# Sliding-window attention with Q/K stacks in two tiles: the second tile holds tokens 768 to 2047 instead of 1024 to 2047

## The chip, the cores and the metric

The kernel is one program on one core of one Trainium2 chip. The metric is device time in microseconds (us) of one execution. Three executions of the kernel before took 1101.31, 1106.22 and 1108.74 us; their median is 1106.22.

## The reference

One transformer block on 2048 tokens of width 640: attention with 32 heads of 20 over a sliding window of 256 tokens, then a gated MLP that also mixes along the sequence. The change concerns the attention.

```
h = layernorm(x); q, k, v = split(h @ wqkv)            # 32 heads, Dh = 20
scores = q @ k.T * Dh ** -0.5
mask = (i - j >= 0) & (i - j < 256)                    # query i, key j
o = softmax(where(mask, scores, -1e9)) @ v
h = x + o @ wo
z = gelu(layernorm(h) @ w_in); z1, z2 = halves(z); g = w_sp @ layernorm(z2) + b_sp
out = h + (z1 * g) @ w_out
```

## The kernel before, in words

**Stages.** The span has four: normalization, V, Q and K (0 to about 239 us), attention (about 239 to 468 us), output projection with the second normalization, and the MLP, whose products on TensorE fill the rest.

**Q and K in pieces.** Q and K are f32 values that must keep their accuracy, so `split_qk` (lines 603 to 620) cuts each into three bf16 parts on ScalarE, VectorE and GpSimd and stores them with one DMA for each (m, c) into the DRAM tensor `qk_d`: m (0 to 9) counts blocks of 128 rows of Q and K, c (0 to 3) blocks of 512 tokens. Two bf16 tokens travel as one f32 word.

**Stacks.** A group g is four heads; there are eight. For a group `load_stack` (lines 316 to 330) fills a stack: the six products of parts that matter are laid on 6 x 20 = 120 partitions, so one bf16 matmul over 120 rows gives the f32 score. A stack has two SBUF tiles: tile 0 holds tokens 0 to 1023, tile 1 tokens 1024 to 2047, each with four heads of Q (index 0) and K (index 1). 12 DMAs of 160 KB fill a tile (line 329). Three stacks (`slot_w`, `slot_ap`) are used in turn; the third lies in the buffers `xb`, which hold the last half of the normalized input until Q and K are done, and the second in memory that the first half held. Before a stack's first use GpSimd sets the K rows 96 to 127 to ones (line 322).

**Maxima and scores.** The program needs the row maximum before the exponential. `max_item(g, qb, hh)` (line 345) computes for one head and 128 queries the scores against up to 384 keys, in four strips of 32 queries with 288 keys each (line 359), and VectorE takes the masked maximum (line 369). In the group 0, which runs in the stage before, it is one product of 128 queries with 384 keys (line 363). `max_rows(g, b)` (line 372) turns the maxima of eight query blocks with a product (line 375), cuts them into three bf16 rows on VectorE and GpSimd, stores them to the DRAM tensor `m_d` (line 384) and loads them into the partitions 120 to 122 of the stack's Q, tile b (line 386). `score_item(u, hh)` (line 391) computes, transposed, the scores of 128 keys with the 384 queries that see them, less the maxima, over 123 rows (line 412), ScalarE takes the exponential (line 415), GpSimd clears the two triangles outside the window (lines 419 and 422), and `pv_item` (line 425) multiplies by V (line 440).

**Spans over two tiles.** `tokens` (line 332) cuts a span of keys or queries that crosses token 1024 into two pieces, each with its weight load and its matmul. For each head this is so in the query blocks 8 and 9 of the maxima and in the key blocks 6 and 7 of the scores: four strips each, so 16 more weight loads and 16 more matmuls a head. The columns streamed are the same, 288 a strip.

**Order.** The attention loop (line 760) is written out by hand: step s computes the four heads of max block s + 16 and of score block s, with PV of block s - 2 between them. A group is 16 steps. SP issues all DMAs in program order; the loads of the stack for two groups ahead are spread over a group's 16 steps, tile 0 first. PE, VectorE and ScalarE also keep program order; GpSimd's order is chosen by the scheduler of the framework.

Of the kernel before, what the change touches and what calls it, by code (L numbers as in the profile page):

```python
# [7 lines left out]
F32 = mybir.dt.float32  # L8
# [26 lines left out]
def block_kernel(ctx, tc, x, xt, wqk, wv, wo, w_in, wsp, bsp, w_out, out):  # L35
# [220 lines left out]
    with ExitStack() as ab:  # L256
# [21 lines left out]
        add_slot(0, s0)  # L278
        add_slot(2, [h[:, :2 * S] for h in xb])
        mask = tmp2.tile([P, 384], BF16, name="mask")  # L280
# [35 lines left out]
        def load_stack(g):  # L316


            st = slot_w[g % 3]
            if g < 3:  # L320
                for h in st:
                    nc.gpsimd.memset(h[96:P, 1], ONES)
                    if g == 2:
                        yield
            for b in range(2):
                for j, parts in enumerate(((0, 0), (0, 1), (0, 2), (1, 0), (1, 1), (2, 0))):
                    for a in range(2):
                        src = qk_d[g // 4, parts[a], b, a * DH:(a + 1) * DH, g % 4 * 4:g % 4 * 4 + 4]
                        nc.sync.dma_start(st[b][j:6 * DH:6, a], src)
                        yield  # L330

        def tokens(st, rows, a, hh, t0, n):

            o = 0
            while o < n:
                c, t = divmod(t0 + o, S // 2)
                w = min(n - o, S // 2 - t)
                yield o, w, st[c][:rows, a, hh, t:t + w]
                o += w

        def one(st, rows, a, hh, t0, n):
            (_, _, x), = tokens(st, rows, a, hh, t0, n)
            return x

        def max_item(g, qb, hh, strips=True):

            st = slot_ap[g % 3]
            ps = s1_tile()
            lo = max(0, qb - 2) * P
            n = (qb + 1) * P - lo  # L350
            keep = mask[:, 384 - n:]
            if strips:
                skip = 32 if qb > 1 else 0
                if skip:
                    n, keep = 288, strip
                for j in range(4):
                    q0 = qb * P + 32 * j
                    for o, w, k in tokens(st, 120, 1, hh, lo + skip * j, n):
                        nc.tensor.matmul(ps[32 * j:32 * j + 32, o:o + w], one(st, 120, 0, hh, q0, 32), k,  # L359
                                         start=True, stop=True, tile_position=(0, 32 * j))  # L360
            else:
                for o, w, k in tokens(st, 120, 1, hh, lo, n):
                    nc.tensor.matmul(ps[:, o:o + w], one(st, 120, 0, hh, qb * P, P), k, start=True, stop=True)  # L363
# [27 lines left out]
        def score_item(u, hh):  # L391
# [14 lines left out]
            for i in range(4):  # L406
                k0 = kb * P + 32 * i
                b, e = 32 * i, min(n, 32 * i + 288)
                if NU - LEAD < u and 4 * (u - NU + LEAD - 1) + hh < 6:
                    b, e = 0, n  # L410
                for o, w, q in tokens(st, 123, 0, hh, kb * P + b, e - b):
                    nc.tensor.matmul(ps[32 * i:32 * i + 32, b + o:b + o + w], one(st, 123, 1, hh, k0, 32), q,  # L412
                                     start=True, stop=True, tile_position=(0, 32 * i))
            if u <= NU - LEAD:
# [50 lines left out]
        if True:  # L465
# [137 lines left out]
            def split_qk(m, c, ps):  # L603
# [10 lines left out]
                else:  # L614
                    nc.scalar.activation(sg[:, 1, :], rest, AF.Copy)  # L615
                nc.gpsimd.tensor_tensor(out=sg[:, 2, :], in0=rest, in1=sg[:, 1, :], op=OP.subtract)  # L616
                T = S // 4
# [103 lines left out]
            def dense_tail():  # L721
                split_wqk(8)
                split_wqk(9)
                for n, (m, c) in enumerate((m, c) for c in range(4) for m in (6, 7, 8, 9)):
# [3 lines left out]
                    if n == 7:  # L728
                        x01.close()
                        s1 = pool(x01, "slot1p", side="right")  # L730
                        add_slot(1, [s1.tile([P, 2 * S], F32R, name=f"slot1_{i}") for i in range(2)])
                    if n >= 7:
# [830 lines left out]
```

## Time and profile before

| what | value |
|---|---|
| median of three executions | 1106.22 us |
| the profiled execution | 1106.83 us, of which its span 1105.1 us |
| mean granted TensorE clock | 0.998 |
| attention steps: 245 to 445 us | PE busy 188.92, VectorE 183.95, ScalarE 178.65, GpSimd 135.68 of 200 us |
| end of attention: 445 to 470 us | PE 22.93, ScalarE 20.73, GpSimd 20.97 of 25 us |
| the rest: 553 to 1105 us | PE 543.51 of 552 us |
| DMA in 245 to 445 us | 35.62 MB, 16 engines busy 0.57 of the time |

PE stands for TensorE's matmuls and PEld for its weight loads, DVE for VectorE, ACT for ScalarE, POOL for GpSimd, SP for the engine that issues DMAs. An x with a number is a count. In brackets behind a row stands how long the engine was idle before it and what released it; "issue" means that the engine waited for nothing that the profile shows. A matmul's end is modelled, so consecutive matmuls overlap in the rows, and idle time of PE is counted from the modelled end.

### The profile page before, as it was taken

The numbers are of one execution on the slowest core, as the hardware profiler recorded it, in microseconds if no ns is written. First come the engines' busy times: TensorE is split into PE (matmuls) and PEld (weight loads), VectorE is DVE, ScalarE is ACT, GpSimd is POOL, SyncE is SP. The second block draws the span as 40 slices with busy tenths as digits, with TensorE's granted clock in tenths as the row PEclk, the third lists the DMA queues.
The fourth block names the chain that finished last, engine by engine and source line by source line (L and its number), as shares of the span: only waits on it lengthen the run. The fifth ranks groups of instructions, "written<-read, shape, count | busy, mean of one in ns | idle before, by whom it ended". The sixth has DMA issues, their size and how long they took to land.

```text
span 1105.1 us, 28802 instructions
## 1 busy us (share of the span) xinstructions
PE 1075.1 (97%) x11083; PEld 970.4 (88%) x11083; DVE 781.6 (71%) x2157; ACT 604.1 (55%) x1258; POOL 314.3 (28%) x447
## 2 busy tenths in 40 slices
PE   8999999999999999999999999999999999999998
PEld 7998887668777788699999999999999899999998
DVE  6643444789899999576677669655456899987784
ACT  4443443249888899846766556443448533333331
POOL 4324446677666676811300012000001000000000
PEclk9999999999999999999999999999999999999999
DMA  7833567555555555689654442242441467684642
GB/s 249 299 115 118 175 173 273 166 166 187 183 183 182 176 178 163 167 267 311 247 200 153 152 142 76 64 132 95 134 147 51 166 229 249 234 272 142 191 145 96
DMA packets 92282, 194.74 MB, mean 176 GB/s; under 512 B 11952, under 2 KB 46272, under 8 KB 88256
## 3 DMA queue, kind: packets, MB, share of 16 engines
q1 hardware_dynamic: 92144, 192.90, 53.5%
q8 instruction: 87, 1.43, 0.5%
q14 instruction: 51, 0.42, 0.1%
HBM read 127.90 MB, written 64.95 MB: 175 GB/s over the span
## 4 chain that ended last, share of the span: by engine, by line
PE 43%; DMA 4%; issue 4%; ACT 3%; DVE 3%; POOL 2%; SPq 0%; ACTq 0%; POOLq 0%; DVEq 0%
PE g L1181 23%; PE zb L1066 4%; PE out_x L1345 3%; PE zx L1006 2%; PE out_v L1345 2%; PE zv L1006 2%; DMA h_d<-xh 1%; PE zy L1006 1%; PE zw L1006 1%; PE out_y L1345 1%; PE yt L1300 1%; DMA fx<-wsp_in 1%; DVE row L822 1%; PE wo_ps L118 1%; ACT pt L417 1%
## 5 line engine op out<-in xcount | busy, mean ns | idle before, releaser
L415 ACT ACTIVATE pt<-bank 128x384 f32<-128x384 f32 (+1 forms) x452 | 179.7, 485 | 22.6 <-PE bank L412 18.5
L1181 PE MATMUL g<-zl,aw 128*128 128x432 f32 x768 | 168.9, 357 | 0.7 <-ACT zl L828 0.7
L369 DVE CUSTOM_DVE_ANT_0 junk<-bank,strip 128x288 bf16<-128x288 f32 x392 | 157.1, 452 | 14.9 <-PE bank L359 12.9
L828 ACT ACTIVATE aw<-fx 128x512 fp32r<-128x512 f32 (+2 forms) x152 | 86.0, 586 | 128.3 <-PE g L1181 53.5
L1181 PEld LDWEIGHTS g<-zl,aw 128*128 128x128 f32 x768 | 144.0, 188 | 7.0 <-ACT zl L828 1.1
L822 DVE TENSOR_TENSOR aw<-fx,aw 128x512 fp32r<-128x512 f32 (+2 forms) x152 | 95.9, 639 | 59.4 <-ACT aw L828 59.1
L440 PE MATMUL pv<-pt,v_sb 128*32 128x192 f32 (+3 forms) x1984 | 134.3, 323 | 3.3 <-issue 1.3
L1181 PE MATMUL g<-ze,aw 128*128 128x432 f32 x576 | 132.6, 359 | 2.3 <-DVE row L822 2.3
L1181 PEld LDWEIGHTS g<-ze,aw 128*128 128x128 f32 x576 | 107.1, 188 | 9.0 <-DVE row L822 3.7
L359 PE MATMUL bank<-slot 120*32 120x288 bf16 (+5 forms) x1280 | 95.9, 277 | 4.2 <-issue 2.5
L419 POOL TENSOR_SCALAR_AFFINE_SELECT pt<-pt 128x512 f32<-128x512 f32 x128 | 81.7, 639 | 56.7 <-ACT pt L415 53.5
L412 PE MATMUL bank<-slot 123*32 123x288 bf16 (+6 forms) x1296 | 96.8, 275 | 0.7 <-ACT pt L415 0.7
L412 PEld LDWEIGHTS <-slot 123*32 123x32 bf16 x1728 | 61.2, 97 | 13.5 <-issue 3.7
L422 POOL TENSOR_SCALAR_AFFINE_SELECT pt<-pt 128x512 f32<-128x512 f32 x112 | 72.8, 650 | 0.0
L440 PEld LDWEIGHTS pv<-pt,v_sb 128*32 128x32 f32 x1984 | 63.1, 110 | 10.4 <-POOL pt L419 4.8
L359 PEld LDWEIGHTS <-slot 120*32 120x32 bf16 x1440 | 51.7, 96 | 16.4 <-issue 9.6
L822 DVE TENSOR_TENSOR row<-g,row 128x432 f32<-128x432 f32 x80 | 48.4, 605 | 21.5 <-PE g L1181 21.1
L369 DVE CUSTOM_DVE_ANT_0 junk<-bank,mask 128x384 bf16<-128x384 f32 (+2 forms) x120 | 51.2, 447 | 16.8 <-PE bank L363 15.6
L616 POOL TENSOR_TENSOR sg<-rest,sg 128x512 bf16<-128x512 f32 x40 | 46.7, 1168 | 56.9 <-ACT sg L615 46.3
L606 DVE TENSOR_TENSOR rest<-qk,std 128x512 f32<-128x512 f32 x40 | 27.6, 690 | 47.8 <-PE qk L594 47.8
L608 ACT ACTIVATE sg<-rest 128x512 bf16<-128x512 f32 x40 | 25.2, 631 | 53.5 <-DVE rest L606 53.5
L118 PE MATMUL wo_ps<-xb,xb 128*128 128x320 f32 x260 | 52.4, 311 | 1.4 <-DVE mvc L1460 1.4
(263 smaller groups left out, 2528.1 us busy)
## 6 DMA issues: line engine op xcount, KB each, us to landing
slot<-qk_d SPq DMA_DIRECT2D x144, 160.0 KB
fx<-wsp_in SPq DMA_DIRECT2D x32, 512.0 KB
qk_d<-sg SPq DMA_DIRECT2D x40, 384.0 KB
o_d<-ot SPq DMA_DIRECT2D x64, 128.0 KB
xb<-qk_d SPq DMA_DIRECT2D x48, 160.0 KB
fx<-hn_d SPq DMA_DIRECT2D x24, 320.0 KB
z_d<-row SPq DMA_DIRECT2D x16, 432.0 KB
g_d<-row SPq DMA_DIRECT2D x16, 432.0 KB
```

Of the source, the lines that this page charges most:

```text
L359: nc.tensor.matmul(ps[32 * j:32 * j + 32, o:o + w], one(st, 120, 0, hh, q0, 32), k, start=True, stop=True, tile_position=(0, 32 * j))
L369: nc.vector.tensor_tensor_reduce(out=junk[:, :n], in0=ps[:, :n], in1=keep, scale=1.0, scalar=NEG, op0=OP.add, op1=OP.max, accum_out=m_cols ...
L412: nc.tensor.matmul(ps[32 * i:32 * i + 32, b + o:b + o + w], one(st, 123, 1, hh, k0, 32), q, start=True, stop=True, tile_position=(0, 32 * i))
L415: nc.scalar.activation(pt[:, hh, :n], ps[:, :n], AF.Exp, scale=SCALE)
L419: nc.gpsimd.affine_select(out=pt[:, :, :P], in_=pt[:, :, :P], pattern=[[0, 4], [1, P]], base=0, channel_multiplier=-1, compare_op=OP.is_ge ...
L422: nc.gpsimd.affine_select(out=pt[:, :, 256:], in_=pt[:, :, 256:], pattern=[[0, 4], [-1, P]], base=-1, channel_multiplier=1, compare_op=OP. ...
L440: nc.tensor.matmul(ps[32 * hh:32 * hh + 32, a - 512 * c:b - 512 * c], v_sb[:, kb, v0:v0 + 32], pt[:, hh, a - kb * P:b - kb * P], start=fir ...
L822: (eng or nc.vector).tensor_tensor(out=out, in0=a, in1=b, op=op)
L828: nc.scalar.activation(out, a, AF.Copy)
L1006: nc.tensor.matmul(ps, a[x], b[:, y], start=start and m + x + y == 0, stop=stop and m == n - 1 and x == 1, skip_group_check=True)
L1181: nc.tensor.matmul(ps, w[m][:, x, k], zc[k][m][:, y], start=start and k + x + y == 0, stop=stop and k == 3 and x == 1, skip_group_check=True)
L1345: nc.tensor.matmul(o[b][:, :HD], l[:, x, k * P:(k + 1) * P], r[k][:, y], start=start and k + x + y == 0, stop=stop and k == 2 and x == 1, ...
```

## The change

`qk_d` becomes two DRAM tensors: the first holds tokens 0 to 1023 (512 words), the second tokens 768 to 2047 (640 words). The second tile of each stack has 1280 tokens instead of 1024. Each span of keys or queries now lies in one tile: maxima use tile 0 for query blocks 0 to 7 and tile 1 from block 8, scores tile 0 for key blocks 0 to 5 and tile 1 from block 6. Tokens 768 to 1023 are stored, loaded and kept twice: `split_qk` stores the c = 1 blocks with two DMAs (ten more DMAs in all), the 12 loads of tile 1 carry 200 KB each, the maxima of query blocks 6 and 7 are loaded into both tiles (eight more DMAs), and the memset of tile 1 covers 2560 columns instead of 2048.

```diff
-    qk_d = dram.tile([2, 3, 2, 2 * DH, H // 2, S // 4], F32, name="qk_d")
+    WORDS = (S // 4, S // 4 + P)
+    qk_d = [dram.tile([2, 3, 2 * DH, H // 2, n], F32, name=f"qk_d{b}") for b, n in enumerate(WORDS)]
...
-        s0 = [s0.tile([P, 2 * S], F32R, name=f"slot0_{i}") for i in range(2)]
+        s0 = [s0.tile([P, 8 * n], F32R, name=f"slot0_{i}") for i, n in enumerate(WORDS)]
...
-        def tokens(st, rows, a, hh, t0, n):
-
-            o = 0
-            while o < n:
-                c, t = divmod(t0 + o, S // 2)
-                w = min(n - o, S // 2 - t)
-                yield o, w, st[c][:rows, a, hh, t:t + w]
-                o += w
-
-        def one(st, rows, a, hh, t0, n):
-            (_, _, x), = tokens(st, rows, a, hh, t0, n)
-            return x
+        def one(st, b, rows, a, hh, t0, n):
+            t = t0 - 6 * P * b
+            return st[b][:rows, a, hh, t:t + n]
...
+            half_b = qb // 8
...
-                    for o, w, k in tokens(st, 120, 1, hh, lo + skip * j, n):
-                        nc.tensor.matmul(ps[32 * j:32 * j + 32, o:o + w], one(st, 120, 0, hh, q0, 32), k,
-                                         start=True, stop=True, tile_position=(0, 32 * j))
+                    nc.tensor.matmul(ps[32 * j:32 * j + 32, :n], one(st, half_b, 120, 0, hh, q0, 32),
+                                     one(st, half_b, 120, 1, hh, lo + skip * j, n),
+                                     start=True, stop=True, tile_position=(0, 32 * j))
...
-            nc.sync.dma_start(slot_w[g % 3][b][120:123, 0], rows.rearrange("a (h r) c -> a h (r c)", h=4))
+            rows, st = rows.rearrange("a (h r) c -> a h (r c)", h=4), slot_w[g % 3]
+            if b == 0:
+                nc.sync.dma_start(st[0][120:123, 0], rows)
+                nc.sync.dma_start(st[1][120:123, 0, :, :P], rows[:, :, 6 * P // 2:])
+            else:
+                nc.sync.dma_start(st[1][120:123, 0, :, P:], rows)
...
-                for o, w, q in tokens(st, 123, 0, hh, kb * P + b, e - b):
-                    nc.tensor.matmul(ps[32 * i:32 * i + 32, b + o:b + o + w], one(st, 123, 1, hh, k0, 32), q,
-                                     start=True, stop=True, tile_position=(0, 32 * i))
+                c = int(kb > 5)
+                nc.tensor.matmul(ps[32 * i:32 * i + 32, b:e], one(st, c, 123, 1, hh, k0, 32),
+                                 one(st, c, 123, 0, hh, kb * P + b, e - b),
+                                 start=True, stop=True, tile_position=(0, 32 * i))
...
-                base = qk_d[m // 5, 0, c // 2, m % 5 * 8, 0, c % 2 * 256:c % 2 * 256 + 256]
-                nc.sync.dma_start(bass.AP(tensor=base.tensor, offset=base.offset,
-                                          ap=[[T, P], [2 * 2 * DH * H // 2 * T, 3], [1, 256]]), sg.bitcast(F32))
+                for b in range(2):
+                    t0, t1 = max(c * 256, 3 * P * b), min(c * 256 + 256, (3 * P + WORDS[1]) if b else WORDS[0])
+                    if t0 >= t1:
+                        continue
+                    o = t0 - 3 * P * b
+                    base = qk_d[b][m // 5, 0, m % 5 * 8, 0, o:o + t1 - t0]
+                    nc.sync.dma_start(bass.AP(tensor=base.tensor, offset=base.offset,
+                                              ap=[[WORDS[b], P], [2 * DH * H // 2 * WORDS[b], 3], [1, t1 - t0]]),
+                                      sg[:, :, 2 * (t0 - c * 256):2 * (t1 - c * 256)].bitcast(F32))
```

The first place where the instruction order differs is PE at key block 6 of group 1, head 0, in the attention loop; `bank` is a PSUM bank, `slot_0_1953` and `slot_1_1954` are the two tiles of the stack (`slot_1_1964` is tile 1 of the changed program), 32 is the strip's keys and the last number the streamed columns. Before:

```order
L412 LDWEIGHTS slot_0_1953
L412 MATMUL bank_124<-slot_0_1953 32x256
L412 LDWEIGHTS slot_0_1953
L412 MATMUL bank_124<-slot_1_1954,slot_0_1953 32x32
L412 LDWEIGHTS slot_0_1953
L412 MATMUL bank_124<-slot_0_1953 32x224
L412 LDWEIGHTS slot_0_1953
L412 MATMUL bank_124<-slot_1_1954,slot_0_1953 32x64
```

These are two of the head's four strips. In the changed program the same head is this:

```order
L410 LDWEIGHTS slot_1_1964
L410 MATMUL bank_125<-slot_1_1964 32x288
L410 LDWEIGHTS slot_1_1964
L410 MATMUL bank_125<-slot_1_1964 32x288
L410 LDWEIGHTS slot_1_1964
L410 MATMUL bank_125<-slot_1_1964 32x288
L410 LDWEIGHTS slot_1_1964
L410 MATMUL bank_125<-slot_1_1964 32x288
```

All four strips now take eight instructions where they took sixteen. Over the whole program PE has 976 instructions fewer: 488 weight loads and 488 matmuls.

The second place is GpSimd at the end of the stage before attention, where it splits the last blocks of Q and K (`rest`, `sg`) and sets the ones of the third stack's second tile (`xb_98` before, `xb_99` in the changed program). Before:

```order
L616 TENSOR_TENSOR sg_3_2268<-rest_3_2269,sg_3_2268 128x512
L322 MEMSET xb_98 32x2048
L610 TENSOR_TENSOR rest_3_2311<-rest_3_2311,sg_3_2310 128x512
L381 CAST m_0_1_2356<-mr_1_2357 32x128
L613 CAST sg_3_2310<-rest_3_2311 128x512
```

And in the changed program:

```order
L323 MEMSET xb_99 32x2560
L615 TENSOR_TENSOR sg_3_2272<-rest_3_2273,sg_3_2272 128x512
L609 TENSOR_TENSOR rest_3_2315<-rest_3_2315,sg_3_2314 128x512
L374 CAST m_0_1_2360<-mr_1_2361 32x128
L612 CAST sg_3_2314<-rest_3_2315 128x512
```

The memset is a quarter larger and stands one instruction earlier, ahead of the split of the last block but one.

The third place is SP where the maxima of the first eight query blocks of group 1 come back from DRAM. Before there is one load, `L386 DMA slot_0_1953<-m_d 3x2048`; in the changed program there are two:

```order
L381 DMA slot_0_1963<-m_d 3x2048
L382 DMA slot_1_1964<-m_d 3x4x128
```

SP has 18 DMAs more in all: these eight and the ten second stores of `split_qk`.

More of the change, by code (lines that the diff above doesn't have):

```diff
@@ L278, in block_kernel @@
         add_slot(0, s0)
-        add_slot(2, [h[:, :2 * S] for h in xb])
+        add_slot(2, [h[:, :8 * n] for h, n in zip(xb, WORDS)])
         mask = tmp2.tile([P, 384], BF16, name="mask")
@@ L327, in load_stack @@
                     for a in range(2):
-                        src = qk_d[g // 4, parts[a], b, a * DH:(a + 1) * DH, g % 4 * 4:g % 4 * 4 + 4]
+                        src = qk_d[b][g // 4, parts[a], a * DH:(a + 1) * DH, g % 4 * 4:g % 4 * 4 + 4]
                         nc.sync.dma_start(st[b][j:6 * DH:6, a], src)
                         yield
-        def tokens(st, rows, a, hh, t0, n):
-            o = 0
-            while o < n:
-                c, t = divmod(t0 + o, S // 2)
-                w = min(n - o, S // 2 - t)
-                yield o, w, st[c][:rows, a, hh, t:t + w]
-                o += w
-        def one(st, rows, a, hh, t0, n):
-            (_, _, x), = tokens(st, rows, a, hh, t0, n)
-            return x
+        def one(st, b, rows, a, hh, t0, n):
+            t = t0 - 6 * P * b
+            return st[b][:rows, a, hh, t:t + n]
         def max_item(g, qb, hh, strips=True):
@@ L357, in max_item @@
                     q0 = qb * P + 32 * j
-                    for o, w, k in tokens(st, 120, 1, hh, lo + skip * j, n):
-                        nc.tensor.matmul(ps[32 * j:32 * j + 32, o:o + w], one(st, 120, 0, hh, q0, 32), k,
-                                         start=True, stop=True, tile_position=(0, 32 * j))
-            else:
-                for o, w, k in tokens(st, 120, 1, hh, lo, n):
-                    nc.tensor.matmul(ps[:, o:o + w], one(st, 120, 0, hh, qb * P, P), k, start=True, stop=True)
+                    nc.tensor.matmul(ps[32 * j:32 * j + 32, :n], one(st, half_b, 120, 0, hh, q0, 32),
+                                     one(st, half_b, 120, 1, hh, lo + skip * j, n),
+                                     start=True, stop=True, tile_position=(0, 32 * j))
+            else:
+                nc.tensor.matmul(ps[:, :n], one(st, half_b, 120, 0, hh, qb * P, P), one(st, half_b, 120, 1, hh, lo, n),
+                                 start=True, stop=True)
             b, c = divmod(qb, 8)
@@ L616, in split_qk @@
                 nc.gpsimd.tensor_tensor(out=sg[:, 2, :], in0=rest, in1=sg[:, 1, :], op=OP.subtract)
-                T = S // 4
-                base = qk_d[m // 5, 0, c // 2, m % 5 * 8, 0, c % 2 * 256:c % 2 * 256 + 256]
-                nc.sync.dma_start(bass.AP(tensor=base.tensor, offset=base.offset,
-                                          ap=[[T, P], [2 * 2 * DH * H // 2 * T, 3], [1, 256]]), sg.bitcast(F32))
+                for b in range(2):
[7 more added lines that the diff above has]
+                                      sg[:, :, 2 * (t0 - c * 256):2 * (t1 - c * 256)].bitcast(F32))
             halves = [slice(0, HD), slice(HD, D)]
@@ L730, in dense_tail @@
                         s1 = pool(x01, "slot1p", side="right")
-                        add_slot(1, [s1.tile([P, 2 * S], F32R, name=f"slot1_{i}") for i in range(2)])
+                        add_slot(1, [s1.tile([P, 8 * n], F32R, name=f"slot1_{i}") for i, n in enumerate(WORDS)])
                     if n >= 7:
```

## The prediction

> **What bounds the kernel now.** I read the page first, then the stretches of the attention stage, then who waited for whom there, then the single waits.
>
> ```profile
> span 1105.1 us, 28802 instructions
> PE 1075.1 (97%) x11083; PEld 970.4 (88%) x11083; DVE 781.6 (71%) x2157; ACT 604.1 (55%) x1258; POOL 314.3 (28%) x447
> q8 instruction: 87, 1.43, 0.5%
> ```
>
> PE is busy nearly throughout, so a matmul saved should count. The third row is a DMA queue that moves no data of the program: 87 packets, 1.43 MB, 16.4 KB each. PE has 11083 + 11083 recorded instructions; divided by 87 that is 255. I read the queue as PE's own code, in blocks of 256 instructions. The change removes 976 of them, almost four blocks, all in the attention stage or just before it.
>
> ```profile
> 245.00:345.00 100.00, 94.02 (x2883) 79.57 (x2879) 91.83 (x466) 88.98 (x232) 69.05 (x120) 1.00 0.58 182
> 345.00:445.00 100.00, 94.91 (x2860) 80.72 (x2853) 92.12 (x468) 89.67 (x238) 66.63 (x115) 1.00 0.57 174
> q8 instruction: 45, 0.74, 1.6%
> ```
>
> The columns are the stretch, its length, then busy time and count of PE, PEld, DVE, ACT, POOL, the clock, the DMA share and GB/s; the last row is the code queue in 245 to 445 us. Three engines are busy nine tenths of this stage, so it has no single bound: work taken from PE alone soon meets VectorE (184 of 200 us). A wait that stops PE, though, is lost for all, since VectorE and ScalarE have no slack to catch up with. 45 blocks are consumed here in 200 us, one in 4.4 us.
>
> ```profile
> PE bank L359 <- issue: 6.3, 6, 1.8
> PE pv L440 <- issue: 1.3, 2, 0.8
> PE bank L412 <- DMA slot<-m_d: 1.2, 1, 1.2
> PE bank L412 <- issue: 0.2, 1, 0.2
> ```
>
> These are PE's waits in 245 to 445 us (total, times, longest). Nine of them, 7.8 us, have no releaser. Five of the nine:
>
> ```profile
> 276.95 0.43 PE L440 MATMUL pv<-pt,v_sb 128*32 128x128 f32 x8 [0.82 <-issue]
> 313.01 0.23 PE L359 MATMUL bank<-slot,slot 120*32 120x160 bf16 x1 [1.83 <-issue]
> 344.19 0.24 PE L359 MATMUL bank<-slot 120*32 120x192 bf16 x1 [1.27 <-issue]
> 375.95 0.30 PE L359 MATMUL bank<-xb 120*32 120x288 bf16 x1 [1.60 <-issue]
> 428.98 0.22 PE L359 MATMUL bank<-slot 120*32 120x96 bf16 x1 [1.01 <-issue]
> ```
>
> Counting instructions between consecutive waits of the nine shows what they are:
>
> ```profile
> 276.50:312.00 35.50, 32.70 (x1018) 28.23 (x1018) 31.89 (x163) 31.23 (x82) 23.82 (x41) 1.00 0.58 179
> 312.00:339.05 27.05, 25.79 (x765) 21.27 (x765) 24.83 (x128) 24.13 (x64) 18.04 (x32) 1.00 0.58 179
> 339.05:343.50 4.45, 3.67 (x126) 3.35 (x126) 4.00 (x19) 3.60 (x9) 3.19 (x7) 1.00 0.69 248
> 348.70:375.00 26.30, 24.97 (x764) 21.18 (x763) 24.35 (x125) 23.82 (x63) 18.40 (x33) 1.00 0.58 179
> ```
>
> PE and PEld together: 2036, 1530, 252 and 1527, that is 8, 6, 1 and 6 times 256, a few records missing. PE stops only where a code block ends: the next has not landed. All but the first lie in the steps in which spans are cut (query blocks 8 and 9, key blocks 6 and 7) or directly behind them, where code is used up fastest:
>
> ```profile
> 251.15:258.18 7.03, 7.03 (x258) 6.26 (x250) 6.99 (x36) 6.73 (x18) 5.60 (x11) 1.00 0.68 226
> 258.18:264.96 6.78, 6.78 (x206) 6.00 (x199) 6.63 (x34) 6.71 (x18) 4.82 (x8) 1.00 0.54 173
> ```
>
> The first row is the four cut steps of group 0, the second the four after them, neither with a stop: 508 instructions in 7.03 us against 405 in 6.78 us. A block lasts 3.5 us in the one and 4.3 us in the other.
>
> The Trainium skill ("Runtime: NRT & Kernel Launch", section Instruction fetch mechanics) says that code is refilled in 16 KiB blocks of 256 instructions, and that crossing a block's boundary is mostly hidden. The trace agrees on the block. It does not on the hiding, with 1.83 us at one boundary; by the rule the next term would be 0 and the sum 0.7 us above the profiled time.
>
> **The change part by part.** All sums are against the profiled execution, 1106.83 us (its span and 1.7 us around it), 0.6 us over the median of the three shown.
>
> (1) *Waits for code.* Uncut, the blocks of the cut steps last 0.8 us longer (4.3 less 3.5), time in which a late block can land. A wait of more than 0.8 us loses 0.8, a smaller one goes. The four large ones above give 3.2 us, the four small ones of cut steps all they have (7.8 less 0.82, 1.83, 1.27, 1.60 and 1.01: 1.3 us), together 4.5 us. The other bound takes the uncut stretches as they are: the cut steps of seven groups use 7 x 508 / 256 = 14 blocks, which leaves 31, and one of these stopped, for 0.82 us. 41 blocks at that rate wait 1.1 us, and 6.7 us go. I take the middle, about **-5.5 us** (0 if the waits move on, below; -7.8 if all go).
>
> (2) *The matmuls themselves.* The columns stay, so only what a piece costs beyond its columns can be saved. Two pairs of heads, from the first maximum to PV, one uncut, one with both scores cut:
>
> ```profile
> 272.80 0.31 PE L359 MATMUL bank<-xb 120*32 120x288 bf16 x4
> ...
> 273.30 0.35 PE L440 MATMUL pv<-pt,v_sb 128*32 128x192 f32 x4
> 281.89 0.37 PE L359 MATMUL bank<-xb 120*32 120x288 bf16 x4
> ...
> 282.40 0.33 PE L440 MATMUL pv<-pt,v_sb 128*32 128x192 f32 x1
> ```
>
> 0.50 us against 0.51 us with eight matmuls more. Over four steps the two rows above differ by 0.25 us, part of which is the product of line 375, that only the first stretch has. So a group saves 0 to 0.25 us, seven groups 0 to 1.75 us, and VectorE, busy 6.63 of the uncut 6.78 us, lets little more through. I take **-0.7 us**, nearer the pair.
>
> (3) *Wider loads.*
>
> ```profile
> DMA packets 15392, 35.62 MB, mean 178 GB/s; under 512 B 4075, under 2 KB 11166, under 8 KB 12406
> slot<-qk_d SPq DMA_DIRECT2D x96, 160.0 KB
> xb<-qk_d SPq DMA_DIRECT2D x48, 160.0 KB
> ...
> 306.63 3.69 SPq L329 DMA_DIRECT2D slot<-qk_d  x5
> ```
>
> The first three rows are of 245 to 445 us, the last a burst of SP's issues. Half of these 144 loads grow by a quarter. They run two groups ahead, and the list of PE's waits above has none for them. But code blocks are fetched by DMA too, and the engines are 0.57 busy. The loads are 23.6 of the 35.6 MB; a quarter more on half of that is 8%, a share of 0.62. Five loads issued in 3.69 us are 222 GB/s, and 278 in a burst for tile 1. If a code block lands 0.1 us later for it, four or five blocks at the edge lose that: **+0.5 us** (0 to 6, the rival below). The eight extra loads of maxima and ten extra stores go through SP, which is not waited for: line 386 made PE wait once, for 1.2 us, at the load for the second eight query blocks, whose place in SP's order stays.
>
> (4) *The memset ahead of the split.*
>
> ```profile
> 236.73 1.16 POOL L616 TENSOR_TENSOR sg<-rest,sg 128x512 bf16<-128x512 f32 x1 [0.74 <-ACT sg L615]
> 237.94 1.80 POOL L322 MEMSET xb<- 32x2048 f32 x1
> 239.82 1.16 POOL L610 TENSOR_TENSOR rest<-rest,sg 128x512 f32<-128x512 f32 x1
> 243.40 0.63 POOL L419 TENSOR_SCALAR_AFFINE_SELECT pt<-pt 128x512 f32<-128x512 f32 x1
> L322 POOLq EVENT_SEMAPHORE x4: 17/17/17, 85.5 to 237.2; - x4
> 244.08 0.55 PE L440 MATMUL pv<-pt,v_sb 128*32 128x192 f32 x4
> ```
>
> The memset overwrites input that the last Q/K product reads, so it can't start before that ends, which the wait at 237.2 us shows. Now it stands ahead of the split that ran at 236.73, and that split waits too: 237.2, plus 1.80 x 2560/2048 = 2.25, plus 1.16, is 240.6 us where the same two were done at 239.74. GpSimd then works without a gap to the first triangle at 243.40, for which PE's first PV waits (244.08). So **+0.9 us**, 0 if PE's other waits at this change of stages cover it.
>
> Sum: -5.5 - 0.7 + 0.5 + 0.9 = -4.8 us, 1102.0 us against the profiled run; the median lies 0.6 us lower: **1101.5 us**. What follows is PE's own work, so what is saved before it stays saved:
>
> ```profile
> 553.00:1105.00 552.00, 543.51 (x2957) 519.53 (x2955) 397.10 (x762) 252.17 (x489) 18.48 (x32) 1.00 0.46 153
> ```
>
> **The rivals.**
>
> *All code waits go* (chance 0.12). Uncut blocks might last long enough everywhere, and the 1.2 us for maxima, which follows directly on a code wait at 276.95, goes as well: -7.8 - 1.2 - 0.7 + 0.9 = -8.8, some 1097.5 us. Against it: that wait is in an uncut step.
>
> *Each piece costs a fixed time* (0.06). If a piece cost what an uncut strip takes from start to start, 0.50 us by 16 = 31 ns, 448 pieces in seven groups would save 14 us; half of it, beside the code waits, is 1106.8 - 7 - 4.8 = 1095 us. For it speaks PE's 97%, against it the 0.51 us above. The Trainium skill ("TensorEngine Tiling (Array Packing)", section Instruction Overhead) has the rule: each matmul has about 60 cycles of overhead, and one of a single column takes as long as one of 60. At the 2.4 GHz of the Trainium skill ("TensorE: Matmul & The Clock Gate", Part 1), 488 matmuls would give 12.2 us, an estimate from these two pages. The trace disagrees: eight more pieces, four of them of 32 to 128 columns, cost 0.01 us.
>
> *The waits for code only move* (0.24). A block may be late because of what the DMA engines do at that moment, not because PE is fast. Then 41 blocks have the rate of the 45 now, 7.1 us of waits: -0.7 - 0.7 + 0.5 + 0.9 = 0, 1106.5 us. The wait at 276.95 in an uncut step speaks for it, the other eight against it. The Trainium skill's sentence on hidden boundaries (as above) would end near here as well, and the trace's 7.8 us speak against its reason, not against the result.
>
> *The wider loads hold up the code* (0.10), the side on which it gets slower. Place: the bursts of five loads for tile 1, in the second half of every group. If code packets queue behind 278 GB/s where they queued behind 222, each of 41 blocks may land up to 1 us later. It decides from 0.8 us, where the time gained by uncut steps is spent: the eight waits then stay, and if every fourth other block waits 0.5 us, that is 5 us more: 1106.5 + 5 + 0.7 = 1112 us. Against it: even at a share of 0.62 the engines are free over a third of the time.
>
> **How the numbers follow.** My forecast has 0.48, within 1098 to 1105 us. The range reaches to the rivals on both sides: from 1094.5 (near the case of fixed costs) to 1108.5 us (beyond the case in which waits move), with about 2 in 10 outside. One per cent, 11 us, is about what a measurement of this kernel can tell from no change (the three executions lie 7 us apart). Faster by over 1% needs under 1095.2 us: fixed costs and the lower edge of the case in which all waits go, 0.13. Slower by over 1% is the far part of the last rival, 0.05. Within 1%: 0.82.
>
> **What would show it.** Right: PE has 976 instructions fewer and 83 or 84 code blocks; in the attention stage one to five waits without a releaser remain, at whole multiples of 256 instructions, 1 to 4 us in all; the four formerly cut steps of a group take 6.8 us; the first triangle of GpSimd comes about 0.9 us later after the last Q/K product. Wrong: nine or more such waits (they only moved), cut and uncut steps that differ by over 0.5 us without a stop (fixed costs), or waits in the steps in which tile 1 is loaded (the wider loads).

## The result, and the profile after

The changed kernel takes **1119.66 us** (median of six, 1116.11 to 1120.97), the kernel before 1108.29 us beside it (six, 1101.31 to 1110.8): ratio 1.011, 95% interval 1.0083 to 1.0137. It is slower by 1.1%, above the predicted range of 1094.5 to 1108.5 us. The profiled execution took 1120.88 us. Two executions on record stand far outside the others and are in no ratio below: 2719.04 us, one of ten of the run with neither width nor extra row load, and 1310.67 us, one of the kernel before.

First the page after: span, PE, code queue.

```profile
span 1119.2 us, 27850 instructions
PE 1079.4 (96%) x10595; PEld 968.5 (87%) x10595; DVE 783.1 (70%) x2157; ACT 604.4 (54%) x1258; POOL 315.4 (28%) x447
q8 instruction: 83, 1.36, 0.5%
```

488 matmuls and as many weight loads are gone, and four code blocks. PE's busy share still fell. The same two stretches of the attention as shown of before, after:

```profile
245.00:345.00 100.00, 89.48 (x2472) 73.52 (x2472) 86.71 (x438) 84.22 (x219) 65.10 (x113) 0.98 0.55 181
345.00:445.00 100.00, 92.69 (x2523) 75.88 (x2527) 88.42 (x446) 85.83 (x223) 65.15 (x114) 0.97 0.58 186
```

PE, VectorE and ScalarE each work 7 to 9 us less in these 200 us than before, so all three wait for something else, and the clock is 0.98 and 0.97 where it was 1.00. PE's waits after for rows of maxima, and those without a releaser, in 245 to 455 us (total, times, longest):

```profile
PE bank L410 <- DMA slot<-m_d: 8.0, 4, 3.5
PE bank L410 <- DMA xb<-m_d: 5.4, 2, 3.4
PE bank L410 <- issue: 1.6, 2, 1.2
PE pv L439 <- issue: 0.3, 1, 0.3
```

The waits for code, 7.8 us before, are 1.9 us. But PE waits six times, 13.4 us, for the rows of maxima (`m_d`) at key block 6, where before it waited once, for 1.2 us. The third in length (3.45, 3.39 and 3.38 us lead), on PE:

```profile
310.28 0.31 PE L351 MATMUL bank<-slot 120*32 120x288 bf16 x4
313.96 0.31 PE L410 MATMUL bank<-xb 123*32 123x288 bf16 x4 [3.38 <-DMA xb<-m_d]
...
315.14 0.49 PE L410 MATMUL bank<-xb 123*32 123x288 bf16 x4
315.38 0.89 PE L439 MATMUL pv<-pt,v_sb 128*32 128x192 f32 x8
```

What it waits for starts on GpSimd, which finishes cutting these maxima at 301.64 + 0.42 = 302.06 us, and goes on in SP's queue:

```profile
301.64 0.42 POOL L375 TENSOR_TENSOR m<-mr,m 32x128 bf16<-32x128 f32 x1
```

```profile
303.28 2.31 SPq L330 DMA_DIRECT2D slot<-qk_d  x3
306.31 0.32 SPq L377 DMA_DIRECT2D m_d<-m  x1
306.96 1.49 SPq L330 DMA_DIRECT2D slot<-qk_d  x2
308.56 0.41 SPq L461 DMA_DIRECT2D o_d<-ot  x1
310.88 0.73 SPq L384 DMA_DIRECT2D xb<-m_d  x1
```

SP stores the maxima at 306.31, 4.26 us after they are there: it is still at the loads of Q and K that stand ahead. It issues two more loads and a store, then stands still until the store of maxima has landed, and issues the load of the rows at 310.88. PE has them at 313.96. The same place before:

```profile
299.39 0.42 POOL L382 TENSOR_TENSOR m<-mr,m 32x128 bf16<-32x128 f32 x1
```

```profile
301.29 0.40 SPq L384 DMA_DIRECT2D m_d<-m  x1
301.78 1.46 SPq L329 DMA_DIRECT2D slot<-qk_d  x2
303.33 0.42 SPq L462 DMA_DIRECT2D o_d<-ot  x1
305.01 0.27 SPq L386 DMA_DIRECT2D xb<-m_d  x1
```

There the store goes out 1.48 us after its data, and the load follows 3.72 us behind it, not 4.57. Over the 13 stores between 250 and 445 us SP is late by 0.67 us on average before (0.03 us in eight of them), by 1.72 us after.

What issuing the loads costs SP, in ns, in 245 to 455 us (smallest/median/largest, first and last start): two rows of before, three of after, and one of the kernel before with a dummy load (an experiment below), in which all loads of Q and K carry 160 KB.

```profile
L386 SPq DMA_DIRECT2D slot<-m_d x11: 265/271/277, 246.4 to 447.4; - x11
L329 SPq DMA_DIRECT2D slot<-qk_d x96: 694/702/1152, 272.1 to 415.3; - x96
```

```profile
L384 SPq DMA_DIRECT2D slot<-m_d x5: 727/735/742, 247.4 to 434.0; - x5
L382 SPq DMA_DIRECT2D slot<-m_d x5: 734/737/762, 265.4 to 445.1; - x5
L330 SPq DMA_DIRECT2D slot<-qk_d x96: 707/716/1212, 274.3 to 428.9; - x96
```

```profile
L330 SPq DMA_DIRECT2D slot<-qk_d x96: 707/714/2301, 273.8 to 422.5; - x96
```

A group costs SP 0.74 us more for the load that was added (L382), and 0.46 us more for the second row load, which no longer fills whole rows of its tile (0.27 before, 0.73 now). The loads of Q and K show 0.716 us after and 0.702 before, but the last row has 0.714 with 160 KB throughout, so the width itself adds nothing that can be seen to what SP issues. SP's waits for the store of maxima, in the same window, before and after:

```profile
SPq L386 <- DMA m_d<-m: 20.3, 15, 3.2
```

```profile
SPq L384 <- DMA m_d<-m: 15.8, 7, 3.2
SPq L381 <- DMA m_d<-m: 13.2, 7, 2.9
```

29.0 us instead of 20.3 us. SP's issues add up to 145.9 us of this window's 210 us before and to 153.5 us after. Together with these waits, which stand in the middle of an ordered queue, that is 166.2 and 182.5 us; waits for buffers and for output tiles come on top.

Along the span: the first PV comes 1.1 us later (245.21 against 244.08 us); the attention's steps 0 to 112 take 213.5 us instead of 203.8; what follows the last PV takes 637.2 us instead of 633.6.

### The profile page after: what moved, and what is told of

The parts are those of the page before. It is cut to its first block, busy times and chain, and to the rows that moved or that the text cites. A ratio compares the mean times of both kernels' runs of the same rounds, so it can differ in the third digit from the quotient of the medians.

```text
span 1119.2 us, 27850 instructions
## 1 busy us (share of the span) xinstructions
PE 1079.4 (96%) x10595; PEld 968.5 (87%) x10595; DVE 783.1 (70%) x2157; ACT 604.4 (54%) x1258; POOL 315.4 (28%) x447
## 4 chain that ended last, share of the span: by engine, by line
PE 42%; DMA 5%; DVE 4%; ACT 4%; issue 3%; POOL 1%; SPq 0%; ACTq 0%; DVEq 0%; POOLq 0%
PE g L1185 22%; PE zb L1070 4%; PE out_x L1349 3%; PE zx L1010 2%; PE out_v L1349 2%; PE zv L1010 2%; PE zy L1010 1%; PE zw L1010 1%; PE yt L1304 1%; PE out_y L1349 1%; ACT pt L416 1%; DMA m<-o_d 1%; DVE row L826 1%; PE wo_ps L119 1%; DMA y_d<-row 1%
## 5 line engine op out<-in xcount | busy, mean ns | idle before, releaser
L410 PE MATMUL bank<-slot 123*32 123x288 bf16 (+5 forms) x1296 | 94.7, 282 | 10.2 <-DMA slot<-m_d 8.0
L351 PE MATMUL bank<-slot 120*32 120x288 bf16 (+2 forms) x1280 | 95.3, 287 | 2.0 <-DMA slot<-qk_d 1.2
L410 PEld LDWEIGHTS <-slot 123*32 123x32 bf16 x1536 | 53.6, 97 | 24.9 <-DMA slot<-m_d 8.4
L362 DVE CUSTOM_DVE_ANT_0 junk<-bank,mask 128x384 bf16<-128x384 f32 (+2 forms) x120 | 51.0, 447 | 17.2 <-PE bank L355 15.4
L351 PEld LDWEIGHTS <-slot 120*32 120x32 bf16 x1280 | 45.9, 96 | 12.5 <-issue 4.4
```

The costliest lines, as they stand in the source:

```text
L351: nc.tensor.matmul(ps[32 * j:32 * j + 32, :n], one(st, half_b, 120, 0, hh, q0, 32), one(st, half_b, 120, 1, hh, lo + skip * j, n), start=T ...
L410: nc.tensor.matmul(ps[32 * i:32 * i + 32, b:e], one(st, c, 123, 1, hh, k0, 32), one(st, c, 123, 0, hh, kb * P + b, e - b), start=True, sto ...
```

## The experiments

The theory (Q in the expectations): SP's in-order queue sets the pace. Issue times and two waits for a store's landing fill a group; what the change adds makes it late with the rows, and TensorE, freed of the cuts, waits at key block 6. Rivals: P, that TensorE only arrives too early; B, that the bytes ahead of the rows hold them up; S, that the cuts cost nothing and SP's order is all.

All runs in one table. Attention is the time from step 0 to step 112 (first exponentials); rows is PE's waits for maxima, code its waits without a releaser, store SP's waits for the store of maxima (all in 245 to 455 us, summed over the rows of the waits); late is by how much SP issues that store after GpSimd has its data, mean of the 13 or 14 stores in 250 to 445 us.

| run | median us | ratio to before (95%) | attention | rows | code | store | late |
|---|---|---|---|---|---|---|---|
| before | 1105.5 to 1108.3 (medians beside the runs) | 1 | 203.8 | 1.2 | 7.8 | 20.3 | 0.67 |
| after | 1119.66 | 1.011 (1.0083 to 1.0137) | 213.5 | 13.4 | 1.9 | 29.0 | 1.72 |
| DMA part alone | 1119.3 | 1.0108 (1.0078 to 1.0139) | 213.9 | 7.8 | 7.1 | 27.1 | 1.40 |
| neither width nor extra row load | 1113.18 | 1.0047 (1.0026 to 1.0067) | 205.6 | 8.6 | 1.7 | 23.3 | 2.23 |
| width alone | 1116.7 | 1.009 (1.0058 to 1.0122) | 209.7 | 10.8 | 1.9 | 28.9 | 1.78 |
| extra row load alone | 1114.47 | 1.0074 (1.0051 to 1.0096) | 207.7 | 11.9 | 0.6 | 23.0 | 2.19 |
| before with a dummy load | 1113.68 | 1.0065 (1.004 to 1.0091) | 208.5 | 9.6 | 3.1 | 19.9 | 2.68 |
| after, rows one step later | 1104.26 | 0.9974 (0.9951 to 0.9997) | 196.9 | 3.5 | 0.4 | 12.8 | 0.60 |
| after, rows two steps later | 1108.96 | 1.0022 (1.0004 to 1.0041) | 205.7 | 11.8 | 0.7 | 0 | 0.32 |
| before, rows two steps later | 1111.75 | 1.0053 (1.0032 to 1.0074) | 207.0 | 7.1 | 3.2 | 0 | 0.03 |
| before, rows one step later | 1106.32 | 0.9997 (0.9978 to 1.0017) | 198.9 | 0 | 4.1 | 3.6 | 0.07 |
| DMA part alone, rows one step later | 1107.87 | 1.0 (0.9982 to 1.0018) | 200.7 | 1.4 | 3.5 | 10.9 | 0.58 |
| after, rows ahead of their step's load | 1115.96 | 1.0089 (1.0065 to 1.0112) | 208.5 | 10.2 | 1.6 | 22.2 | 1.70 |
| after, one step later, store sooner | 1107.02 | 0.9995 (0.9977 to 1.0012) | 202.0 | 0 | 4.3 | 17.2 | 0.46 |

**The DMA part alone.** The changed stores, tiles and loads, with the matmuls cut at token 1024.

```diff
-                nc.tensor.matmul(ps[32 * i:32 * i + 32, b:e], one(st, c, 123, 1, hh, k0, 32),
-                                 one(st, c, 123, 0, hh, kb * P + b, e - b),
+                for o, w, q in tokens(st, 123, 0, hh, kb * P + b, e - b):
+                    nc.tensor.matmul(ps[32 * i:32 * i + 32, b + o:b + o + w], one(st, 123, 1, hh, k0, 32), q,
...
```

> The change's stores, 640-token second tiles and split row loads, but the matmuls cut at token 1024 as before the change. Theory Q (SP's queue is late with the rows of maxima, because it carries the extra and longer loads; TensorE then waits for them at key block 6): the waits at key block 6 stay, several of 1 to 4 us, and the time is 1117 to 1126 us, at or above the change's 1119.7, with the nine waits at code blocks back. Rival P (TensorE, freed of the cuts, only arrives too early for rows that are not later than they were): with the cuts back the time returns to 1107 to 1110 us and no wait at key block 6 is over 1 us.

1119.3 us, no different from the change. Its PE waits:

```profile
PE bank L419 <- DMA slot<-m_d: 7.4, 4, 2.5
PE bank L419 <- DMA xb<-m_d: 0.4, 1, 0.4
PE bank L361 <- issue: 4.0, 4, 2.5
PE bank L419 <- issue: 1.7, 2, 1.0
PE pv L447 <- issue: 1.4, 3, 0.8
```

The waits for code are back (7.1 us), the waits for rows are shorter by about as much (7.8 instead of 13.4), and the attention takes 213.9 us, after 213.5. That is how it looks when another queue sets the pace: what PE loses in one place it would have waited for in another. Rival P falls, and as far as the times can tell the whole loss belongs to the DMA part.

**Neither, the width alone, the extra row load alone.** From group 3 on, the second tile's loads are left at 1024 tokens (from step 24), the extra row load is left out (from step 40, five loads), or both.

```diff
-                        src = qk_d[b][g // 4, parts[a], a * DH:(a + 1) * DH, g % 4 * 4:g % 4 * 4 + 4]
-                        nc.sync.dma_start(st[b][j:6 * DH:6, a], src)
+                        w = P * (b and g > 2)
+                        src = qk_d[b][g // 4, parts[a], a * DH:(a + 1) * DH, g % 4 * 4:g % 4 * 4 + 4, w:]
+                        nc.sync.dma_start(st[b][j:6 * DH:6, a, :, w:], src)
...
-                nc.sync.dma_start(st[1][120:123, 0, :, :P], rows[:, :, 6 * P // 2:])
+                if g < 3:
+                    nc.sync.dma_start(st[1][120:123, 0, :, :P], rows[:, :, 6 * P // 2:])
```

> The changed kernel, but from group 3 on the second tile loads only tokens 1024 to 2047 (1024 wide, as before the change) and the extra row load is left out; its tokens 768 to 1023 and their maxima stay those of the group three before, so the outputs of heads 12 to 31 are not the reference's. Theory Q: the waits at key block 6 go in groups 2 to 6 (11.1 us of gaps and about 4.7 us of slower clock behind them), the one of group 1 stays: 1103 to 1108 us. Rival P: the waits stay and the time is 1116 to 1121 us.

> The changed kernel without the extra row load from group 3 on (so the maxima of tokens 768 to 1023 in the second tile are those of the group three before); the wide loads stay. If SP's issue time is what counts (0.74 us of it less per group), most of what e2_both gains is gained here: 1104 to 1111 us. If the bytes of the wide loads ahead of the store of maxima count, little is: 1114 to 1120 us. Rival P: 1116 to 1121 us.

> The changed kernel with the second tile's loads 1024 tokens wide from group 3 on (its tokens 768 to 1023 are then those of the group three before); the extra row load stays. If the bytes of the wide loads ahead of the store of maxima count, most of what e2_both gains is gained here: 1104 to 1111 us. If SP's issue time counts, little is: 1114 to 1120 us. Rival P: 1116 to 1121 us.

Without the extra row load (3.7 us of SP's issues in all) the attention is 3.8 us shorter than after, without the width 5.8, without both 7.9. Each counts, the width more: by the medians it takes 5.2 us of the 6.5 us that both take, the extra load 3.0. The gains were smaller than expected: the run without both was to take 1103 to 1108 us and takes 1113.18, and each of the other two, at 1116.7 and 1114.47 us, lies in the range that was given for a gain of little. The width acts though it does not visibly lengthen what SP issues: with it SP waits 28.9 to 29.0 us for its stores to land, without it 23.0 to 23.3. So theory Q has to take in a part of B: with the width a load of rows starts 4.1 us (after) or 4.0 us (width alone) behind its store, on average over 15 stores, without it 3.5 (neither) and 3.6 us (extra row load alone); wider loads delay the small store's landing, and SP stands still for that. And the run without both still has waits for rows of 8.6 us, and is about 5 us slower than the kernel before (0.47%): the first groups, which keep width and extra load, and the longer second row load may be a part of that; how much is not shown. A faster PE alone did not get past SP's queue there.

**One dummy load in the kernel before.**

```diff
...
+            nc.sync.dma_start(spare[120:123], rows.rearrange("a (h r) c -> a h (r c)", h=4)[:, :, :P])
```

> The kernel before the change with one more load on SP behind each row load (3 partitions x 4 x 128 words of the same maxima into a tile that nobody reads): 0.74 us of SP twice a group and 6 KB, the rest as before. Theory Q: SP's round grows by 1.5 us a group, from about 28.2 to 29.7, over TensorE's 29.1: 1110 to 1118 us, with waits at key block 6. Rival B: 6 KB are nothing, 1105 to 1109 us.

Nothing changes in the computation, in TensorE's program or in the loads of Q and K; 6 KB are loaded that nobody reads, for 0.74 us of SP twice a group. The dummy's row, and PE's waits:

```profile
L388 SPq DMA_DIRECT2D spare<-m_d x15: 713/739/757, 246.9 to 453.0; - x15
```

```profile
PE bank L414 <- DMA slot<-m_d: 5.1, 3, 1.9
PE bank L414 <- DMA xb<-m_d: 4.5, 2, 2.4
```

Theory Q had 1110 to 1118 us, rival B 1105 to 1109; it is 1113.68. SP is late by 2.68 us on average, and PE waits 9.6 us for rows, with the cuts and without a wider load anywhere. 1.48 us of SP per group, 10.4 us in seven, cost 4.7 us of attention, though the waits for code are 4.7 us shorter. SP's queue had little room even before the change.

**The row loads one or two steps later in SP's order.** SP issues loads of Q and K instead of waiting for the store.

```diff
-                if hh == 3 and u1 % 8 == 1 and s <= NU - LEAD + 1:
+                if hh == 3 and u1 % 8 == 2 and s <= NU - LEAD + 2:
```

> The changed kernel, its row loads one step later in SP's order: between the change and e5_late. Theory Q: half of SP's waits for the store go (1 to 2 us of room per group), most waits at key block 6 go: 1100 to 1109 us. Rival B: 1119 to 1125 us.

> The changed kernel, its row loads two steps later in SP's order, so that SP issues the three loads of Q and K that stand between instead of waiting about 3 us for the store of maxima. Theory Q (SP's queue sets the pace of the attention: issue times plus two such waits make its round some 28.5 us and more, TensorE's 27.4 without them): SP gets some 4 to 5 us of room per group, the waits at key block 6 go (14.8 us of gaps, 4.7 us of slow clock), 1098 to 1104 us, under the kernel before. Rival B (the rows are late because of the bytes ahead of them on the DMA engines): three more loads stand ahead of them, the waits grow, 1120 to 1130 us.

> The kernel before the change with the same later row loads: a control. Theory Q: SP's room was just enough there, its nine waits at code blocks (7.8 us) set its round, so it gains the one wait for rows at most: 1104 to 1108 us, 0 to 3 us under the kernel before; and the difference to e5_late is what the cuts cost once SP has room, 5 to 7 us. Rival B: 1106 to 1112 us.

One step later: 1104.26 us, 15 us under the change, with every DMA and every matmul of the change. SP and PE there:

```profile
SPq L384 <- DMA m_d<-m: 8.9, 8, 4.0
SPq L381 <- DMA m_d<-m: 3.9, 4, 1.3
```

```profile
PE bank L410 <- DMA slot<-m_d: 2.6, 3, 1.4
PE bank L410 <- DMA xb<-m_d: 0.9, 2, 0.7
```

SP's waits fall from 29.0 to 12.8 us, PE's for rows from 13.4 to 3.5 us, the granted clock over 245 to 455 us is 1.00 again:

```profile
245.00:455.00 210.00, 202.14 (x5636) 163.96 (x5640) 187.12 (x938) 194.46 (x493) 151.25 (x260) 1.00 0.61 195
```

In this order the load of rows itself stands as long after its store as in the change (4.0 and 4.1 us on average over 15 stores). It is the store that comes sooner, since SP is not behind. The two-step version was expected to be best, at 1098 to 1104 us without the cuts and 1104 to 1108 with them, and is not: 1108.96 and 1111.75 us. (The second lies in rival B's range, the first far below B's 1120 to 1130.) SP there never waits for the store of maxima; its longest waits are others (this is the kernel after, two steps; L461 is the store of attention outputs `ot`):

```profile
SPq L461 <- DVE ot L460: 14.0, 12, 2.0
```

In between stands the output store of the next step, which can't go before that step's PV is done. SP is punctual (late by 0.32 us), but the load of rows now stands behind a step of PE, 5.3 us after its store on average, and PE waits 11.8 us for it.

**The same loads, cut and uncut, and the kernel before, all with rows one step later.**

> The same stores and loads in the same order as in the run with the row loads one step later (1104.26 us), but the matmuls cut at token 1024 as before the change: only the cuts differ. Theory Q (with room on SP, TensorE sets the pace again, so its instructions count): the nine waits at code blocks are back, 5 to 7 us more, 1108 to 1111 us. Rival S (the cuts cost nothing; all of the gain was SP's order): 1103 to 1106 us.

> The kernel before the change with its row loads one step later and nothing else. Theory Q (before the change TensorE with its waits at code blocks set the pace, SP came just behind): 1104 to 1107 us, next to nothing gained. Rival S (the order of SP's queue held up the kernel before as well): 1099 to 1103 us, as fast as the changed kernel with that order, or faster.

With room on SP the cuts count: the DMA part with cuts takes 200.7 us in the attention, without 196.9, and 1107.87 against 1104.26 us in all; the ratios, 1.0 and 0.9974, have intervals that overlap (from 0.9982, up to 0.9997), so the 3.6 us rests on the two traces as much as on the times. The time lies between the ranges of theory Q (1108 to 1111 us) and rival S (1103 to 1106). Code waits are 3.5 and 0.4 us. The kernel before with this order takes the time that theory Q expected, with an unchanged total (0.9997), but not in the way expected: its attention is 4.9 us shorter, so SP's order had cost it something too, and its profiled execution gives that back behind the attention, where it takes 637.1 us after the last PV instead of 633.6. With this order on both sides, the whole change makes the attention 2.0 us shorter (196.9 and 198.9 us): the sign of the forecast, at less than half its size, and the ratios of the times, 0.9974 and 0.9997, have overlapping intervals.

**Row loads ahead of their step's load.** One step later, but before that step's loads: the only difference to the 1104.26 us is one load of Q and K (two in the first group) that no longer stands between the store and the load of rows.

```diff
+            if s % 8 == 2 and s <= NU - LEAD + 2:
+                next(rows)
             for _ in range(1 + s % 2 if s >= NT else 2 * min(s, 1)):
                 next(ld, None)
...
-                    next(rows)
-                if hh == 3 and u1 % 8 == 1 and s <= NU - LEAD + 1:
                     next(rows)
```

> The changed kernel with the row loads one step later and ahead of that step's load of Q and K instead of behind it: they are issued up to 0.75 us sooner than with one step alone, while SP waits little for the store. Theory Q: the gaps at key block 6 that were left there (0.66, 1.03, 0.89 and 1.70 us) shrink by 1 to 3 us in all, 1101 to 1104 us. Rival S: what SP saves counts alone, 1104 to 1107 us.

A miss, and the clearest run of all: rows that stand one load sooner in the queue make the kernel some 12 us slower (1115.96 and 1104.26 us, ratios 1.0089 and 0.9974). Theory Q had 1101 to 1104 us, rival S 1104 to 1107. In SP's queue this order is the changed kernel's own, but for one output store that goes ahead of every second load of rows, so it takes back most of what one step had gained. SP's waits in it:

```profile
SPq L384 <- DMA m_d<-m: 13.5, 8, 3.2
SPq L381 <- DMA m_d<-m: 8.7, 6, 1.8
```

SP stands still 9.4 us longer than one load further back (22.2 and 12.8 us), and the attention takes 11.6 us longer. In this pair the time in which SP waits is lost about one for one, as it is where the waiting engine sets the pace.

**One step later, with store and extra load moved.**

```diff
-                if hh == 1 and u1 % 8 == 0 and s <= NU - LEAD:
+                if hh == 0 and u1 % 8 == 0 and s <= NU - LEAD:
...
+                if hh == 3 and u1 % 8 == 5 and s <= NU - LEAD + 5:
+                    next(rows, None)
...
```

> The changed kernel with row loads one step later (1104.26 us), and two more moves: the maxima are turned and stored two heads of work sooner in their step, and the extra row load of tokens 768 to 1023, which is not read for another group, is issued three steps behind its partner. Theory Q: the store and the row load go out up to 0.8 us sooner, the gaps left at key block 6 shrink by 1 to 3 us: 1101 to 1104 us. Rival S (nothing is left to gain from rows that are sooner; as in the run with the row loads ahead of their step's load, SP waits instead): 1104 to 1110 us.

1107.02 us, in rival S's range and the same as the kernel before (0.9995). PE no longer waits for rows at all, and yet:

```profile
PE bank L351 <- issue: 3.0, 3, 1.6
PE bank L368 <- DVE mcol L362: 2.0, 7, 0.3
PE bank L411 <- issue: 1.3, 2, 0.8
```

PE now waits for VectorE's last maximum where it turns them, the steps with that product take about 0.25 us longer (14 of them, 3.6 us), and 4.3 us of code waits appear without any cut. The lowest median stays that of the version with rows one step later; the intervals of the two overlap.

## Why the prediction was wrong, point by point

The terms are in the order of the prediction's sum, but the one that failed stands last of the four. (That sum gives 1101.4 us, not 1101.5; nothing hangs on it.)

- **Term (1), waits for code, -5.5 us: right in kind.** Of the nine waits two, not one, lie outside the cut steps: at 276.95 us and, in step 11 of group 3, at 349.02 us (0.48 us); by that the bound of 6.7 us would have been 6.1. After the change 1.9 us are left of 7.8. The pairs that differ in the cuts alone give 7.1 against 1.9 and 3.5 against 0.4, that is -5.2 and -3.1 us. What it rests on is narrower than it said: with no cuts at all the last experiment has 4.3 us of them, and the kernel before with rows one step later has 4.1 us with all its cuts; PE waits for rows in neither. A PE that stops for rows may leave time for a block to land, so that part of the drop is owed to the new waits; no run separates the two.
- **Term (2), the pieces, -0.7 us: about -0.3.** In group 0, where no wait disturbs them, the four formerly cut steps (6 to 9) take 6.98 us after and 7.03 before, 0.05 us a group. The 6.8 us that were to be the sign of a right prediction did not come.
- **Term (4), the memset, +0.9 us: half that.** GpSimd's first triangle starts 6.67 us after the start of the last Q/K matmul before (236.73 to 243.40 us) and 7.11 us after (237.41 to 244.52), and in all the other runs 6.66 to 6.68 with the old memset and 7.11 to 7.13 with the larger one: +0.44 us. That the first PV came 1.1 us later, near the forecast, is luck: 0.68 us of it is that matmul itself, whose start ranges over 1.6 us in the 14 profiles (236.0 to 237.6).
- **Term (3), the wider loads, +0.5 us (0 to 6): the step that failed.** It said that extra loads and stores "go through SP, which is not waited for", because PE waited once and the load of rows keeps its "place in SP's order". The place stayed; its time did not. PE had hardly waited for SP because SP came just in time, not because it had room. The row of before that says so, 20.3 us of waits for the store in SP's queue, has no place in the prediction's working: it goes by PE's waits and the share of the DMA engines, and for SP by one burst. What the runs showed in its place: SP issues 1.2 us more a group for the loads of rows; the wider loads cost it nothing to issue, but the small store behind them lands later; so its waits for the store grow to 29.0 us, it is late with that store by 1.72 us instead of 0.67, and PE waits 13.4 us for rows instead of 1.2. On the attention this term is worth some +15 us, not +0.5: it is 9.7 us longer in all, with 5.9 us of code waits saved beside it. 12.2 us are waits for rows (13.4 less 1.2); about 4.8 us are a slower clock, as behind three of the four longest waits the next two steps took 1.7 to 3.2 us each instead of 1.6 to 1.7. With the code waits saved these come to 11.1 us, an estimate a little above the 9.7 measured.
- **The rival on the slow side (1112 us, chance 0.10) had the sign and the wide loads right, the victim wrong.** The wide loads did hold something up, as their part in the experiments shows (5.8 us of attention), but it was the small store of maxima that SP waits for, not the code; code waits fell in every run with wide loads and no cuts.
- **"What follows is PE's own work, so what is saved before it stays saved": not settled.** Behind the last PV, where the code is the same, the profiled executions take from 633.6 us (before) to 638.0 us (the run with neither width nor extra row load), after 637.2. This is 3.5 of the 14 us between the two spans. It follows neither cuts nor loads (the run with the extra row load alone has 635.8; the three other runs of the kernel before with changed SP orders or a dummy load have 635.2 to 637.1), so the one profile of before may simply be short there; no experiment was made on it, and it stays open.

## What to carry to other kernels

Before you save work on the busiest engine, add up for one round of the loop what each in-order DMA queue issues and how long it stands waiting in the middle; a queue that comes just in time shows no wait on anyone else's list. A load that depends on a store through DRAM makes its queue wait for whatever is left of the landing, unless enough other work stands between the two; where exactly it stood was worth up to 15 us here, more than the change itself, and both one load sooner and one step later were worse than the best place.

## What the runs showed of the hardware

- In these rows a DMA's cost to SP goes by its shape, not its bytes: 0.27 us for 24 KB as 3 whole rows of a tile, 0.73 us for the same 24 KB as 3 x 4 pieces, 0.74 us for 6 KB as 3 x 4 pieces, 0.70 to 0.72 us for loads of Q and K, of 160 or 200 KB. The Trainium skill ("Perfetto Trace Analysis", section What "DMA-bound" means) names the issuing engine's sequencer as one of the things that can bind, recognized by a solid row of DMAs. The trace agrees that it binds; the row here was not solid, about three quarters issue (153.5 of 210 us after), with the waits in between.
- A store of 24 KB and the load that waits for it were 3.4 us apart on average over the 15 stores of the kernel before, whose loads of Q and K carry 160 KB, and 4.1 us with the change, where half of them carry 200 KB. At the two places shown it was 3.7 and 4.6 us; of the three loads just ahead of the store, two carried 200 KB there; the two behind it carried 160 KB.
- Whether the clock falls after a wait does not go by the wait's length alone. Two waits for rows of the changed kernel, on PE:

```profile
282.58 0.31 PE L410 MATMUL bank<-slot 123*32 123x288 bf16 x4 [3.39 <-DMA slot<-m_d]
282.71 0.30 PE L351 MATMUL bank<-xb 120*32 120x288 bf16 x4
...
406.92 0.33 PE L410 MATMUL bank<-xb 123*32 123x288 bf16 x4 [2.00 <-DMA xb<-m_d]
407.04 0.45 PE L351 MATMUL bank<-slot 120*32 120x288 bf16 x4
```

Behind 3.39 us the clock stayed at 1.00; behind 2.00 us it was halved for 3.41 us, and four matmuls took 0.45 us instead of 0.30. In this profile the stretches at half clock begin at 314.92, 376.36 and 407.08 us and last 3.41 us each; they are 18 and 9 times that length apart, so they lie on a grid. The grid's windows around the two waits:

```profile
277.37:280.78 3.41, 1.82 (x56) 1.28 (x44) 2.31 (x12) 2.33 (x7) 2.44 (x4) 1.00 0.55 203
280.79:284.20 3.41, 1.62 (x48) 1.34 (x52) 1.03 (x5) 1.18 (x4) 0.00 (x0) 1.00 0.39 113
...
403.67:407.08 3.41, 1.42 (x44) 0.91 (x39) 1.74 (x10) 1.76 (x5) 2.44 (x4) 1.00 0.33 85
407.08:410.49 3.41, 3.41 (x60) 2.59 (x56) 1.97 (x8) 1.86 (x4) 0.50 (x1) 0.50 0.55 161
```

The wait of 3.39 us was split by the grid, and PE was busy for 1.82 and 1.62 us of the two windows; the wait of 2.00 us lay within one, which left 1.42 us. In the 14 profiles, between 245 and 480 us, every grid window with PE busy for 0 to 1.42 us was followed by one at half clock (12 windows), and none with 1.46 us or more (937). Outside the attention these bounds do not hold: at 241.25 us of the kernel before the clock was halved behind a window with 1.91 us. The Trainium skill ("TensorE: Matmul & The Clock Gate", Part 1) says that the clock is halved after an idle window of about 3.4 us, and that the windows run on their own, not from the wait's start. The second half agrees with these rows; on the first the trace goes further, since here a window did not have to be idle throughout.
